# Seven products in place of eight in the late matrix products of an attention and PReLU kernel

## The chip, the cores and the metric

The kernel runs on one core of one Trainium2 chip. The metric is device microseconds of one execution, the median of several; lower is better. Work on the core is spread over TensorE (PE, matrix products from SBUF into PSUM), VectorE (DVE), ScalarE (ACT), GpSimd (POOL) and the DMA queues that SyncE (SP) and GpSimd feed. Each engine takes its instructions in the order in which the kernel writes them.

## The reference

A block-wise linear attention with a decay per head, and then two matrix products with a PReLU between them. `lam` has a value per head, `alpha` one per hidden column.

```python
# q, k, v: (4, 8, 768, 64); blocks of 64 positions
Dmask = np.where(rel >= 0, lam ** rel, 0.0)
for b in range(nb):
    intra = einsum('bhij,bhjd->bhid', einsum('bhic,bhjc->bhij', qb, kb) * Dmask, vb)
    inter = einsum('bhid,bhde->bhie', qb * lam_pow, kv_state)
    out[:, :, sl] = intra + inter
    kv_state = lam_block * kv_state + einsum('bhsd,bhse->bhde', kb * rev_pow, vb)
x = out.transpose(0, 2, 1, 3).reshape(3072, 512)
h = x @ w_in                                   # 512 -> 2048
g = np.maximum(h, 0.0) + alpha * np.minimum(h, 0.0)
return g @ w_out                               # 2048 -> 512
```

## The kernel before

The 3072 rows are worked in six chunks of 512 (`c` = 0 to 5). A chunk is two batch entries by 256 positions; positions are taken in pairs, so a row index has a part `e` (even or odd position). Attention is done in 24 units (`n`, four to a chunk: batch entry by half of the heads). The kernel works with blocks of 128 positions, two to a chunk.

For a unit: `cast` brings q and k to float16, a transpose by DMA (`transposes(n, "D")`) or by TensorE puts the head dimension on partitions (`qkT`), `decayed` multiplies q by its decay (`qdT`), `key_decayed` does so with k (`kdec`). Then TensorE computes the scores (`score_products`, L387), VectorE multiplies them by the mask (`masked`, L398), TensorE adds the part from the state (`inter`, L371) and the part from the block (`intra`, L412) in the PSUM tile `acc`, ScalarE copies the result to `xT` (`attended`, L248), and the state `R` is brought forward by `state_products` (L432) and VectorE (`states`, L461). `cluster(old, new)` issues these calls for one unit's end and another's beginning.

For a chunk: `up(c, f)` (L532) makes one of 16 groups of 128 hidden columns, four matmuls of 512 columns; ScalarE writes `relu(-h)` to `m` (L540), VectorE computes `g = oma * m + h` from `m` and the PSUM bank (L549), where `oma` is 1 - alpha. `down(c, t, part, 4)` (L562) makes a quarter of the second product for 128 rows, four matmuls of 512 columns; ScalarE copies the finished bank out (L575), SP's queue stores it. `down_last` (L585) is the same for the last chunk, its last tile in pieces of 256, 128 and 128 columns.

Up to chunk 2's first product the order is a written list of calls; from chunk 3 on a string says where `up` (U) and `down` (D) take turns, with attention put between them (`plan`). PSUM has eight banks: two for `acc`, two for the scores, and four named ones: two "h", "tk" and "op". The caller names the bank that a tile takes.

GpSimd runs many casts, most `key_decayed` and `decayed`, and issues the DMAs that load the weights and `v` with a cast to float16 (`load_v16`). SP issues the other loads, the DMA transposes and the stores.

Of the kernel before, what the change touches and what calls it, by code (L numbers as in the profile page):

```python
# [11 lines left out]
def kernel(  # L12
# [26 lines left out]
    L = 128  # L39
# [18 lines left out]
    ps = ctx.enter_context(tc.tile_pool(name="ps", bufs=1, space=bass.MemoryType.PSUM))  # L58
    h_ps_pool = ctx.enter_context(tc.tile_pool(name="hps", bufs=2, space=bass.MemoryType.PSUM))
# [20 lines left out]
    def load(c, bi, x, half=None, queue="S"):  # L80

        pb, b = c // 2, 2 * (c % 2) + bi
        if (c, bi) not in raws:
            raws[c, bi] = [raw_pool.tile([128, H, 2 * D], fp32, tag=f"{n}raw", name=f"{n}raw") for n in "kqv"]
        heads = ds(0, H) if half is None else ds(4 * half, 4)
        i = "kqv".index(x)
        (nc.gpsimd if queue == "G" else nc.sync).dma_start(
            out=raws[c, bi][i][:, heads, :],
            in_=(k, q, v)[i][b, heads, ds(pb * W, W), :].rearrange("h (p e) d -> p h (e d)", e=2),
        )  # L90
# [4 lines left out]
    def load_win(i):  # L95
        nc.gpsimd.dma_start(
            out=w_in_sb[:, :, ts(i, 512)],
            in_=moe_w_in[:, ts(i, 512)].rearrange("(g p) f -> p g f", p=128),
        )

    def load_win8(i):
        nc.gpsimd.dma_start(
            out=w_in_sb[:, :, ts(i, 256)],
            in_=moe_w_in[:, ts(i, 256)].rearrange("(g p) f -> p g f", p=128),
        )
# [24 lines left out]
    def bank_of(bank, name, dtype=fp32):  # L130
        pool = h_ps_pool if bank == "h" else ps
        return pool.tile([128, CH], dtype, tag=bank, name=name)

    def fill(n, bank="h"):

        t = bank_of(bank, "unread")
# [9 lines left out]
    def tick(n, bank="h", x=ident):  # L146

        t = bank_of(bank, "unread")
# [3 lines left out]
    lam_ps = h_ps_pool.tile([128, CH], fp32, tag="h", name="lam_ps")  # L152
    tick(16, "h", zeros[:, 0:128])
# [8 lines left out]
    rel_f = ps.tile([128, CH], fp32, tag="op", name="rel_f")[:, 0:192].rearrange("p (a j) -> p a j", a=3)  # L162
# [71 lines left out]

    def slopes():
        at = h_ps_pool.tile([128, CH], fp32, tag="h", name="at_ps")
        nc.tensor.transpose(at[:, 0:NF], alpha_sb, ident32)
        nc.vector.tensor_scalar(
            out=oma, in0=at[:, 0:NF], scalar1=-1.0, scalar2=1.0, op0=ALU.mult, op1=ALU.add
        )  # L240
# [13 lines left out]
    def raw_of(n):  # L254
        c, bi, hh = units[n]
        return {
            x + "16": t[:, ds(4 * hh, 4), :].rearrange("p h (e d) -> p e h d", e=2)
            for x, t in zip("kqv", raws[c, bi])
        }

    def cast(n, name, eng):
        t = T.setdefault(n, {})
        if name == "v16":
            t[name] = kv_pool.tile([128, 4, 2, D], fp16, tag=name, name=name)
            c, bi, hh = units[n]
            copy_on(eng, t[name].rearrange("p h e d -> p h (e d)"), raws[c, bi][2][:, ds(4 * hh, 4), :])
# [3 lines left out]
        copy_on(eng, t["qk16"][:, int(name == "k16")], raw_of(n)[name])  # L270
# [14 lines left out]
    def key_decayed(n, eng="G"):  # L285
        hh = units[n][2]
        kr = raw_of(n)["k16"]
# [9 lines left out]
    def casts(n, eng):  # L297
        for name, e in zip(("k16", "q16", "v16"), eng):
            cast(n, name, e)
        key_decayed(n)  # L300

    def transposes(n, eng, decay=True):

        t = T[n]
        qkT = qkt_pool.tile([128, 2, 2, 2, L], fp16, tag="qkT", name="qkT")
        if eng == "D":
            nc.sync.dma_start(
                out=qkT.rearrange("p x e h j -> p (x e h) j"),
                in_=t["qk16"].rearrange("p x e h d -> p (x e h d)"),
                transpose=True,  # L310
            )
        else:
            tp = ps.tile([128, 2, 2, 2, L], fp16, tag="tk", name="tp")
            for x in (1, 0):
                for e in range(2):
                    for hp in range(2):
                        nc.tensor.transpose(
                            tp[:, x, e, hp, :],
                            t["qk16"][:, x, e, ds(2 * hp, 2)].rearrange("p l d -> p (l d)"),
                            ident,  # L320
                        )
            copy_on(eng, qkT, tp)
            t["qps"] = tp[:, 0]
        t["qkT"] = qkT
        if decay:
            decayed(n)

    def transposed(n, x, eng, bank):

        c, bi, hh = units[n]  # L330
        t = T.setdefault(n, {})
        if "qkT" not in t:
            t["qkT"] = qkt_pool.tile([128, 2, 2, 2, L], fp16, tag="qkT", name="qkT")
        tp = bank_of(bank, "tpx", fp16).rearrange("p (e h j) -> p e h j", e=2, h=2)
        for e in range(2):
            for hp in range(2):
                nc.tensor.transpose(  # L337
                    tp[:, e, hp, :],
                    t["qk16"][:, x, e, ds(2 * hp, 2)].rearrange("p l d -> p (l d)"),
                    ident,  # L340
                )
        copy_on(eng, t["qkT"][:, x], tp)
        if x == 0:
            t["qps"] = tp
# [80 lines left out]
    def state_products(n, kv, fresh, blocks=None):  # L425
        t = T[n]
        for hp in range(2):
            for e in range(2):
                for hl in range(2):
                    for a in blocks or blocks_of(n):  # L430
                        p = ds(a * 64, 64)
                        nc.tensor.matmul(  # L432
                            kv[a][ds(hl * 64, 64), hp, hl, :],
# [7 lines left out]
    def attended(n, eng):  # L441
        co, bo, ho = units[n]
        if co not in XT:
            XT[co] = xt_pool.tile([128, NHP, 2, 2, L], fp16, tag="xT", name="xT")
# [6 lines left out]
    def states(n, kv, blocks=None):  # L451
        c, bi, hh = units[n]
        pb, b = c // 2, 2 * (c % 2) + bi

        def dense():
            for a in blocks or blocks_of(n):
                m = 2 * pb + a
                if m == 0:
                    continue
                for hp in range(2):  # L460
                    nc.vector.scalar_tensor_tensor(  # L461
                        out=R[b, hh, m + 1][:, hp],
                        in0=R[b, hh, m][:, hp],
                        scalar=rdecay[:, 2 * hh + hp : 2 * hh + hp + 1],
                        in1=kv[a][:, hp],
                        op0=ALU.mult,
                        op1=ALU.add,
                    )

        if pb == 0 and (blocks is None or 0 in blocks):  # L470
            nc.scalar.activation(R[b, hh, 1], kv[0], AF.Copy)
        dense()

    def cluster(old, new, eng="A"):

        if old is not None:
            inter(old)
        if new is not None:
            score_products(new)
        if old is not None:  # L480
            intra(old)
        if new is not None:
            state_products(new, kv_acc, old is None)
            masked(new)
        if old is not None:
            attended(old, eng)
        if new is not None:
            states(new, kv_acc)

    def scores(n):  # L490
        score_products(n)
        masked(n)

    def beside(kv, a):

        p = ds(a * 64, 64)
        for hl in range(2):
            nc.tensor.matmul(
                kv[ds(hl * 64, 64), :, 1 - hl, :],
# [6 lines left out]

    def state(n, pair):

# [583 lines left out]
```

## Time and profile before

| | |
|---|---|
| median of three runs | 210.99 us (210.74 to 211.4) |
| profiled execution, first to last instruction (span) | 209.1 us |
| difference between the two | 1.9 us |
| TensorE busy | 204.0 us, 2151 matmuls |
| VectorE busy | 132.4 us, 233 instructions |
| ScalarE busy | 110.8 us, 207 instructions |
| GpSimd busy | 84.3 us, 114 instructions |

The span is one execution seen by the profiler; the runs' times include what lies around it. A row of a group names the line, the engine, the operation, what it writes from what it reads, the shapes and the count; then the busy time in us, the mean of one instruction in ns, the idle time of the engine just before the group's instructions, and what ended it. A row of the timeline has the start and the length in us. In a stretch's row each engine has its busy us and its count of instructions, and the clock is the share of full speed that TensorE was granted.

### The profile page before, as it was taken

The numbers are of one execution on the slowest core, as the hardware profiler recorded it, in microseconds if no ns is written. First come the engines' busy times: TensorE is split into PE (matmuls) and PEld (weight loads), VectorE is DVE, ScalarE is ACT, GpSimd is POOL, SyncE is SP. The second block draws the span as 40 slices with busy tenths as digits, with TensorE's granted clock in tenths as the row PEclk, the third lists the DMA queues.
The fourth block names the chain that finished last, engine by engine and source line by source line (L and its number), as shares of the span: only waits on it lengthen the run. The fifth ranks groups of instructions, "written<-read, shape, count | busy, mean of one in ns | idle before, by whom it ended". The sixth has DMA issues, their size and how long they took to land.

```text
span 209.1 us, 5240 instructions
## 1 busy us (share of the span) xinstructions
PE 204.0 (98%) x2151; PEld 109.3 (52%) x2151; DVE 132.4 (63%) x233; ACT 110.8 (53%) x207; POOL 84.3 (40%) x114
## 2 busy tenths in 40 slices
PE   7999999999999999999999999999999999999993
PEld 6776455456445465555554464544544444444453
DVE  7978889488789466999956656744674344444000
ACT  7986778154876127666844544643454544344121
POOL 8999793052476983381902938022000000000000
PEclk9999999999999999999999999999999999999999
DMA  6999999998999998999199990404110100111113
GB/s 159 277 197 239 245 253 206 241 282 260 269 211 262 196 241 184 252 209 221 28 220 229 298 211 1 103 0 103 50 48 5 50 39 11 53 52 50 51 50 103
DMA packets 56716, 32.20 MB, mean 154 GB/s; under 512 B 22948, under 2 KB 53044, under 8 KB 56692
## 3 DMA queue, kind: packets, MB, share of 16 engines
q1 hardware_dynamic: 45764, 23.34, 46.4%
q0 software_dynamic: 10912, 8.52, 23.4%
q8 instruction: 17, 0.28, 0.6%
q14 instruction: 7, 0.06, 0.1%
q10 hardware_dynamic: 16, 0.00, 0.0%
HBM read 27.27 MB, written 6.29 MB: 161 GB/s over the span
## 4 chain that ended last, share of the span: by engine, by line
PE 92%; DVE 3%; ACT 2%; issue 1%; ACTq 0%
PE h_ps L532 39%; PE o_ps L562 33%; PE o_ps L585 7%; PE s L387 3%; PE acc L412 2%; PE tpx L337 2%; PE acc L371 2%; DVE dmask L200 1%; PE acc L432 1%; PE acc L629 1%; PE acc L615 1%; ACT qk L248 1%; ACT L178 1%; ACT xT L248 1%; DVE kdec L289 1%
## 5 line engine op out<-in xcount | busy, mean ns | idle before, releaser
L549 DVE SCALAR_TENSOR_TENSOR g<-m,oma,h_ps 128x512 f16<-128x512 f32 (+1 forms) x98 | 71.2, 736 | 46.3 <-ACT m L540 43.3
L532 PE MATMUL h_ps<-xT,w_in_sb 128*128 128x512 f16 (+1 forms) x392 | 91.4, 375 | 0.1
L540 ACT ACTIVATE m<-h_ps 128x512 f32<-128x512 f32 (+1 forms) x98 | 57.3, 588 | 51.0 <-PE h_ps L532 50.5
L562 PE MATMUL o_ps<-w_out_sb,g 128*128 128x512 f16 x320 | 79.0, 379 | 0.0
L532 PEld LDWEIGHTS <-w_in_sb 128*128 128x128 f16 x392 | 37.9, 98 | 43.6 <-issue 0.5
L562 PEld LDWEIGHTS <-g 128*128 128x128 f16 x320 | 29.9, 98 | 34.1 <-DVE g L549 0.2
L398 DVE TENSOR_TENSOR sm<-s,dmask 128x1024 f16<-128x1024 f32 x21 | 25.6, 1221 | 12.4 <-PE s L387 11.7
L351 POOL TENSOR_TENSOR qdT<-qkT,qdecay 128x512 f16<-128x512 f16 (+1 forms) x19 | 20.5, 1083 | 17.3 <-PE h_ps L532 7.2
L248 ACT ACTIVATE xT<-acc 128x512 f16<-128x512 f32 (+1 forms) x27 | 14.2, 550 | 22.6 <-PE acc L432 19.4
L575 ACT ACTIVATE o_sb<-o_ps 128x512 f32<-128x512 f32 (+2 forms) x26 | 14.7, 564 | 15.9 <-PE o_ps L585 10.9
L289 POOL TENSOR_TENSOR kdec<-kraw,kdecay 128x512 f16<-128x512 f32 x18 | 19.7, 1102 | 6.0 <-DMA kraw<-in_k_dram 6.0
L461 DVE SCALAR_TENSOR_TENSOR R<-R,rdecay,acc 128x128 f16<-128x128 f16 x54 | 15.3, 342 | 0.0
L252 POOL CAST qk<-qraw 128x512 f16<-128x512 f32 x12 | 7.4, 614 | 17.1 <-DMA qraw<-in_q_dram 16.2
L252 POOL CAST qk<-kraw 128x512 f16<-128x512 f32 x14 | 8.6, 614 | 13.9 <-DMA kraw<-in_k_dram 10.1
L585 PE MATMUL o_ps<-w_out_sb,g 128*128 128x512 f16 (+2 forms) x96 | 14.1, 308 | 0.0
L585 PEld LDWEIGHTS <-g 128*128 128x128 f16 x96 | 8.1, 98 | 6.1
L387 PE MATMUL s<-qkT 64*64 64x128 f16 x336 | 8.8, 221 | 0.1
L276 POOL DMA_DIRECT2D v<-in_v_dram x11 | 8.6, 792 | 0.0
L248 ACT ACTIVATE qk<-qraw 128x512 f16<-128x512 f32 x11 | 6.9, 624 | 2.7 <-DMA qraw<-in_q_dram 2.1
L252 POOL CAST v<-vraw 128x512 f16<-128x512 f32 x10 | 6.1, 615 | 5.4 <-DMA vraw<-in_v_dram 5.4
L387 PEld LDWEIGHTS <-qkT 64*64 64x64 f16 x336 | 5.8, 106 | 2.1 <-issue 0.4
L248 ACT ACTIVATE qkT<-tpx 128x512 f16<-128x512 f16 x11 | 6.5, 598 | 0.8 <-PE tpx L337 0.8
(76 smaller groups left out, 133.5 us busy)
## 6 DMA issues: line engine op xcount, KB each, us to landing
out_dram<-o_sb SPq DMA_DIRECT2D x23, 256.0 KB, 2.3
kraw<-in_k_dram SPq DMA_DIRECT2D x7, 512.0 KB, 5.6
qraw<-in_q_dram SPq DMA_DIRECT2D x6, 512.0 KB, 5.9
w_in_sb<-in_moe_w_in_dram POOLq DMA_DIRECT2D x4, 512.0 KB, 8.0
w_out_sb<-in_moe_w_out_dram POOLq DMA_DIRECT2D x4, 512.0 KB, 10.6
vraw<-in_v_dram SPq DMA_DIRECT2D x7, 256.0 KB, 5.7
qraw<-in_q_dram POOLq DMA_DIRECT2D x6, 256.0 KB, 7.2
qraw<-in_q_dram SPq DMA_DIRECT2D x6, 256.0 KB, 4.8
```

Of the source, the lines that this page charges most:

```text
L248: nc.scalar.activation(out, in_, AF.Copy)
L252: nc.gpsimd.tensor_copy(out=out, in_=in_)
L289: engine(eng).tensor_tensor(out=kdec, in0=kr, in1=kdecay[:, ds(4 * hh, 4), :].rearrange("p h e -> p e h").unsqueeze(3).to_broadcast([128, ...
L351: engine(eng).tensor_tensor(out=qdT[:, :, :, p], in0=(t["qps"] if eng == "P" else t["qkT"][:, 0])[:, :, :, p], in1=qdecay[:, hh, :, :, p], ...
L387: nc.tensor.matmul(t["s"][ds(a * 64, 64), hl, hp, 1 - e, :].rearrange("p (e j) -> p e j", e=2), lhsT=t["qkT"][p, 1, e, hp, ds(a * 64, 64)] ...
L398: nc.vector.tensor_tensor(out=t["sm"].rearrange("p a h x j -> p (a h) x j"), in0=t["s"].rearrange("p a h x j -> p (a h) x j"), in1=mask_of ...
L461: nc.vector.scalar_tensor_tensor(out=R[b, hh, m + 1][:, hp], in0=R[b, hh, m][:, hp], scalar=rdecay[:, 2 * hh + hp : 2 * hh + hp + 1], in1= ...
L532: nc.tensor.matmul(h_ps[:, 0:n] if bi is None else h_ps[:, 0:n].rearrange("p (e j) -> p e j", e=2), lhsT=w_in_sb[:, gi, ts(f, 128)], rhs=x ...
L540: nc.scalar.activation(m[:, 0:n], h_ps[:, 0:n], AF.Relu, scale=-1.0)
L549: nc.vector.scalar_tensor_tensor(out=g, in0=mv, scalar=oma[:, f : f + 1], in1=hv, op0=ALU.mult, op1=ALU.add)
L562: nc.tensor.matmul(o_ps, lhsT=lhs(c, f, t), rhs=w_out_sb[:, f, :], start=(f == 0), stop=(f == NF - 1),)
L585: nc.tensor.matmul(o_ps[:, 0:n], lhsT=lhs(c, f, t), rhs=w_out_sb[:, f, ds(x, n)], start=(f == 0), stop=(f == NF - 1),)
```

## The change

Up to the end of chunk 0's second product the calls stay in their order. `up` is cut into `up`, `relu` and `prelu`, `down` into `down`, `down_copy` and `down_store`, `cluster` into its calls, so that the list can put each on its own place. From chunk 1's first product on the list is a new one, to the end of the kernel.

PSUM's four named banks become one pool of four (`bank_pool`), from which a tile takes whichever has come free. After the attention `acc` and the scores' banks are given back and make a second pool of four (`late_bank`).

Chunks 2 to 5's second product is done by Strassen's scheme in Winograd's form. A quarter of `g` is eight of the 16 groups (`x`) by one `e` (256 rows); `w_out` is cut into halves by hidden row and by output column. `g_sum` forms the sums of the quarters of `g`, half a quarter (128 x 1024, float16) at a time, eight calls to a chunk, all but one sum in the place of a quarter; `w_sum` forms four sums of quarters of `w_out` (128 x 2048) once. A product `second(c, i, b)` is eight matmuls of 256 columns for 128 rows; seven `i` by two `b` make a chunk. The products are added in two PSUM banks, `a` and `e`; `second_m` copies the first out on ScalarE, `second_m5`, `second_x` and two `second_out` are float32 additions of a PSUM bank and a tile in SBUF on VectorE, two `second_out` are copies on ScalarE. Chunk 5's last product is in pieces (`last`), its final columns 128 wide.

Chunks 4 and 5's first product is done as one, 1024 columns wide: seven products for each of eight pairs of column groups (`first(f, i)`, two matmuls of 512 columns each). `in_sum` and `x_sum` form the sums of quarters of `w_in` and of the two chunks' `xT`, four calls each; per `f` there are two copies on ScalarE (`first_b`, `first_m5`) and two additions on VectorE (`first_x`, `first_d`). `first_d` leaves its sum in SBUF; for seven of the eight `f` the `prelu` that follows is two instructions on GpSimd.

`v` of the units from 16 on is loaded with the cast, and no longer cast by an engine. The sums of weights, of `xT` and of chunk 5's `g` use the places of raw inputs and of weights that are no longer read.

```diff
-    ps = ctx.enter_context(tc.tile_pool(name="ps", bufs=1, space=bass.MemoryType.PSUM))
-    h_ps_pool = ctx.enter_context(tc.tile_pool(name="hps", bufs=2, space=bass.MemoryType.PSUM))
+    bank_pool = ctx.enter_context(tc.tile_pool(name="bank", bufs=4, space=bass.MemoryType.PSUM))
+    ps_stack = ctx.enter_context(ExitStack())
+    ps = ps_stack.enter_context(tc.tile_pool(name="ps", bufs=1, space=bass.MemoryType.PSUM))
...
+    def prelu(c, f, bi=None, eng="V"):
+        g, m, h = g_of(c, f), M[c, f, bi], HP[c, f, bi]
...
+        if eng == "G":
+            nc.gpsimd.tensor_scalar(out=m, in0=m, scalar1=oma[:, f : f + 1], scalar2=None, op0=ALU.mult)
+            nc.gpsimd.tensor_tensor(out=g, in0=m, in1=h, op=ALU.add)
+            return
         nc.vector.scalar_tensor_tensor(
+            out=g, in0=m, scalar=oma[:, f : f + 1], in1=h, op0=ALU.mult, op1=ALU.add
         )
...
+        if i == 1:
+            sub(T_OUT[1], b12, b11, eng)
+        elif i == 2:
+            sub(T_OUT[2], b22, T_OUT[1], eng)
+        elif i == 3:
+            sub(T_OUT[3], b22, b12, eng)
+        else:
+            sub(T_OUT[4], b21, T_OUT[2], eng)
...
+        s1 = S1[c][:, ds(4 * j, 4)]
+        if i == 1:
+            add(s1, a21, a22, eng)
+        elif i == 3:
+            sub(a21, a11, a21, eng)
+        elif i == 2:
+            sub(a11, s1, a11, eng)
+        else:
+            sub(a12, a12, a11, eng)
...
+    def second(c, i, b):
+
+        if i in (1, 5) and b == 0:
+            Y[c, "ae"[i == 5]] = late_bank("y") if c == 5 else bank_of("y")
+        t = Y[c, "ae"[i in (3, 5)]]
+        for f in range(8):
+            nc.tensor.matmul(
+                t[:, ds(b * HALF, HALF)],
+                lhsT=left(c, i, f, b),
+                rhs=right(i, f),
+                start=(f == 0 and b == 0 and i in (1, 5, 6)),
+                stop=(f == 7),
+                skip_group_check=True,
             )
...
+        copy_on("A", Y[c, "m1"], Y[c, "a"])
+
+    def second_m5(c):
+        add(Y[c, "m15"], Y[c, "e"], Y[c, "m1"])
+
+    def second_x(c):
+        add(Y[c, "e"], Y[c, "a"], Y[c, "m15"])
+
+    def second_out(c, i):
+        o = SB[c, i] = o_pool.tile([128, DM], fp32, tag="osb", name="o_sb")
+        if i in (2, 3):
+            copy_on("A", o, Y[c, "ae"[i == 3]])
+        else:
+            add(o, Y[c, "a"], Y[c, "m15" if i == 7 else "m1"])
...
+    def first(f, i):
+
+        k = {1: "a", 2: "a", 5: "e", 3: "e"}.get(i, "b")
+        if i in (1, 5):
+            Q[f, k] = late_bank(k)
+        t = Q[f, k]
...
+        for g in range(2):
+            w, x = both(f, i, g)
+            nc.tensor.matmul(
+                t, lhsT=w, rhs=x, start=(g == 0 and i in (1, 5)), stop=(g == 1), skip_group_check=True
+            )
+
+    def first_b(f):
+        Q[f, "b"] = bank_of("b")
+        copy_on("A", Q[f, "b"], Q[f, "a"])
+
+    def first_m5(f):
+        M5[f] = half_pool.tile([128, CH], fp32, tag="qk16", name="m5")
+        copy_on("A", M5[f], Q[f, "e"])
+
+    def first_x(f):
+        add(Q[f, "e"], Q[f, "b"], M5[f])
+
+    def first_d(f):
+        HP[5, 8 + f, None] = m_pool.tile([128, CH], fp32, tag="m", name="d")
+        add(HP[5, 8 + f, None], Q[f, "b"], M5[f])
...
+    up(3, 9)
+    states(16, (0,))
+    relu(3, 9)
+    second(2, 1, 0)
+    g_sum(2, 1, 1)
+    second(2, 1, 1)
+    masked(17)
+    load_v16(22)
+    prelu(3, 9)
+    up(3, 2)
+    inter(16)
+    g_sum(2, 2, 0)
```

In the stages that the prediction names, chunk 1's second product and chunk 2's first run with units 9 to 16 (to chunk 3's first `up`), chunk 2's second and chunk 3's first with units 16 to 23 (to `first(1, 1)`), the joint first product with chunk 3's second (to `second(4, 1, 0)`), and the second products of chunks 4 and 5 close the kernel.

More of the change, by code (lines that the diff above doesn't have):

```diff
@@ L449, in attended, with kv_of, first_state, states @@
         )
-    def states(n, kv, blocks=None):
+    KV = {}
+    def kv_of(n, a):
+        return KV.get((n, a), kv_acc[a])
+    def first_state(n):
+        c, bi, hh = units[n]
+        nc.scalar.activation(R[2 * (c % 2) + bi, hh, 1], kv_of(n, 0), AF.Copy)
+    def states(n, blocks):
         c, bi, hh = units[n]
         pb, b = c // 2, 2 * (c % 2) + bi
[L455 to L472, printed above, removed]
@@ new lines @@
+    prelu(4, 1)
+    second(3, 1, 0)
+    relu(5, 0)
+    first(1, 6)
+    first(2, 1)
+    second_out(2, 4)
+    second(3, 1, 1)
+    prelu(5, 0)
+    first_b(2)
+    first_d(0)
+    first_x(1)
+    first(2, 2)
+    relu(5, 8)
+    prelu(5, 8, None, "G")
+    first(2, 5)
+    x_sum(4)
+    prelu(4, 0)
+    first_m5(2)
+    first(1, 3)
+    g_sum(3, 1, 1)
+    second_m(3)
+    first(1, 7)
+    relu(5, 1)
+    g_sum(3, 3, 0)
+    first_d(1)
+    prelu(5, 1)
+    first(0, 4)
+    first(3, 1)
+    first(2, 6)
```

1533 lines of the change are left out of this document (1041 added, 492 removed).

## The prediction

> **What bounds the kernel now.** I read the page's totals and chain first, then busy time by stretch, then the chain in order of time, then groups by shape.
>
> ```profile
> span 209.1 us, 5240 instructions
> ...
> PE 204.0 (98%) x2151; PEld 109.3 (52%) x2151; DVE 132.4 (63%) x233; ACT 110.8 (53%) x207; POOL 84.3 (40%) x114
> ...
> PE 92%; DVE 3%; ACT 2%; issue 1%; ACTq 0%
> ```
>
> TensorE is busy for 98% of the span and is 92% of the chain that ended last. VectorE is the next engine. The stretches show where each has room:
>
> ```profile
> core 0: us, PE busy (x) PEld busy (x) DVE busy (x) ACT busy (x) POOL busy (x), PEclk, DMA share, GB/s
> 0.00:52.10 52.10, 50.21 (x740) 31.36 (x741) 41.86 (x83) 34.21 (x69) 35.10 (x56) 1.00 1.17 236
> 52.10:70.40 18.30, 18.30 (x137) 9.07 (x136) 16.01 (x28) 12.19 (x23) 12.79 (x16) 1.00 1.21 251
> 70.40:205.90 135.50, 135.44 (x1276) 68.86 (x1274) 74.50 (x123) 64.16 (x114) 36.44 (x45) 1.00 0.47 112
> 205.90:209.10 3.20, 0.02 (x1) 0.00 (x0) 0.00 (x0) 0.28 (x1) 0.00 (x0) 1.00 0.15 44
> ```
>
> Chunk 1's first product starts at 52.1; the last matmul ends at 205.9; the last copy and store take 3.2. The granted clock is 1.00 throughout. VectorE has 61 of 135.5 us free from 70.4 on.
>
> ```profile
> 82.11 4.32 PE h_ps L532 x20
> ...
> 90.90 0.22 PE acc L371 x4
> 91.12 0.35 PE s L387 x16
> 91.47 0.22 PE acc L412 x16
> 91.69 0.12 PE acc L432 x16
> ...
> 192.03 13.91 PE o_ps L585 x96
> ```
>
> Twenty 512-wide matmuls take 4.32, so 0.216 each and 0.865 for a group of four; one unit of attention takes 0.22 + 0.35 + 0.22 + 0.12 = 0.91. From 52.1 on the old kernel has 80 groups of `up`, 80 of `down` and 16 units: 160 x 0.865 + 16 x 0.91 = 153.0, against 153.8 measured. The stretch is dense; only fewer columns can shorten it.
>
> **TensorE after the change.** L585 is 48 matmuls of 512 columns, 16 of 256 and 32 of 128. With a cost of a per column and b per matmul, 512a + b = 0.216 and 48 x 0.216 + 8192a + 48b = 13.91 give 0.42 ns and 2.7 ns, so 0.109 for 256 columns. Chunks 2 to 5's second products lose 4 x 64 matmuls of 512 (55.3) and get 4 x 112 of 256 (49.0): -6.3. Chunks 4 and 5's first products lose 128 of 512 and get 112: 16 x 0.216 = -3.5. Together -9.8, and a TensorE that never waits would end the span at 199.3.
>
> **What VectorE must do for it.** The page's durations overlap in a row of instructions, so I price by starts:
>
> ```profile
> 85.22 0.68 DVE L351 TENSOR_TENSOR qdT<-qkT,qdecay 128x512 f16<-128x512 f16 x1
> 85.83 2.06 DVE L549 SCALAR_TENSOR_TENSOR g<-m,oma,h_ps 128x512 f16<-128x512 f32 x3
> 87.80 1.22 DVE L398 TENSOR_TENSOR sm<-s,dmask 128x1024 f16<-128x1024 f32 x1
> 88.93 1.12 DVE L461 SCALAR_TENSOR_TENSOR R<-R,rdecay,acc 128x128 f16<-128x128 f16 x4
> 89.96 2.35 DVE L549 SCALAR_TENSOR_TENSOR g<-m,oma,h_ps 128x512 f16<-128x512 f32 x3
> ...
> 98.88 2.72 DVE L549 SCALAR_TENSOR_TENSOR g<-m,oma,h_ps 128x512 f16<-128x512 f32 x4
> ```
> ```profile
> L549 DVE SCALAR_TENSOR_TENSOR g<-m,oma,h_ps 128x512 f16<-128x512 f32 x94 | 69.5, 747 | 46.3 <-ACT m L540 43.3
> L658 DVE TENSOR_TENSOR sm<-s,dmask 128x512 f16<-128x512 f32 x6 | 3.8, 682 | 0.0
> L250 DVE COPY qkT<-tpx 128x512 f16<-128x512 f16 x5 | 1.9, 419 | 0.0
> L250 DVE COPY qkT<-tp 128x1024 f16<-128x1024 f16 x1 | 0.7, 686 | 0.0
> L351 DVE TENSOR_TENSOR qdT<-qkT,qdecay 128x512 f16<-128x512 f16 x1 | 0.7, 684 | 0.0
> L351 DVE TENSOR_TENSOR qdT<-qkT,qdecay 128x256 f16<-128x256 f16 x3 | 1.2, 415 | 0.0
> L351 POOL TENSOR_TENSOR qdT<-qkT,qdecay 128x512 f16<-128x512 f16 x15 | 17.4, 1163 | 17.3 <-PE h_ps L532 7.2 <-DMA qkT<-qk 6.6 <-PE acc L615 3.3
> ```
>
> A prelu costs (2.72 - 0.747)/3 = 0.66, a mask 1.13, a state update 0.26, and the next instruction starts about 0.08 before a long one ends. The new float32 adds from PSUM are like L658: 0.682 - 0.08 = 0.60. The sums of float16 quarters are not in this trace. From above: L351, whose `qdecay` operand is float32, grows by (684 - 415)/256 = 1.05 ns per element, so 1024 elements would take 1.22 and 2048 2.30. From below: the all-float16 copy grows by (686 - 419)/512 = 0.52 ns, so 0.69 and 1.22. The new sums are all float16 with runs of 256 elements or more, so I take the copy's row: 0.60 and 1.14 by starts. [...]
>
> I counted the written order in four stages, marked by calls on TensorE, from `w_sum(1)`, which stands 18.3 of TensorE's work behind 52.1 (at about 70.4):
> - A, to chunk 3's first `up`: TensorE 29 groups and 6 units, 30.7. VectorE 17 prelus 11.2, 7 masks 7.9, 24 state updates 6.2, `w_sum` 1 to 3 3.4, two `g_sum` 1.2, a cast and two decays 1.9: 31.8.
> - B, to `first(1, 1)`: TensorE 16 ups, 13 half products of 0.87, 8 units less a few pieces, 31.2. VectorE 15 prelus 9.9, 7 masks 7.9, 16 updates 4.1, four sums of 2048 4.6, eight of 1024 4.8, three adds 1.8: 33.1.
> - C, to `second(4, 1, 0)`: TensorE 110 matmuls and 15 half products, 36.9. VectorE 22 prelus 14.5, 15 `first_x` and `first_d` 9.1, twelve sums of 1024 and one of 2048 8.3, five adds 3.1: 35.0.
> - D, to `second(4, 4, 0)`, which needs the last `g_sum`: TensorE 17.9. VectorE 14 `g_sum` 8.4, 5 prelus 3.3, seven adds 4.2: 15.9. After it TensorE has 7.0.
>
> The room that was 45% of the stretch is gone. In A and B VectorE has 1.1 and 1.9 more than TensorE, and its queue is in order: a prelu late behind a `w_sum` is late for the bank that the next `up` takes. That adds 3.0. C and D have 1.9 and 2.0 to spare, which covers them; were VectorE's prices 10% higher, A and B would add 3.2 and 3.3 more and C 1.6.
>
> **The port.** The new sums read two operands from SBUF. The old trace has VectorE and GpSimd in each other's way:
>
> ```profile
> 44.53 1.04 POOL L289 TENSOR_TENSOR kdec<-kraw,kdecay 128x512 f16<-128x512 f32 x1 [1.04 <-DMA kraw<-in_k_dram]
> ...
> 46.34 0.61 POOL L252 CAST qk<-qraw 128x512 f16<-128x512 f32 x1 [0.76 <-PE tpx L337]
> ...
> 68.53 1.90 POOL L289 TENSOR_TENSOR kdec<-kraw,kdecay 128x512 f16<-128x512 f32 x1
> ```
> ```profile
> 44.56 1.30 DVE L250 CAST qk<-kraw 128x512 f16<-128x512 f32 x1
> ...
> 46.38 0.84 DVE L250 CAST qk<-kraw 128x512 f16<-128x512 f32 x1
> ```
> ```profile
> L250 DVE CAST qk<-qraw 128x512 f16<-128x512 f32 x1 | 0.4, 419 | 0.0
> L289 DVE TENSOR_TENSOR kdec<-kraw,kdecay x6: 677/682/1148, 5.4 to 68.8; 128x512 f16<-128x512 f32 x6
> ```
>
> A cast of 0.42 took 1.30 and 0.84 where a GpSimd instruction had started just before, and GpSimd's own 1.04 became 1.90 at 68.53. Over 17 such VectorE instructions (6 casts, 6 `kdec`, 5 `qdT`) the loss is 0.88 + 0.42 + 0.47 = 1.8, or 0.10 each. A and B have 17 new sums and so add the same 1.8; C's 13 lose 1.4 inside its 1.9 of room. The bounds are nothing, and 0.88 each time GpSimd computes (the second rival).
>
> **The rest, at nothing.** ScalarE has 19.8, 18.0, 28.7 and 5.4 in the stages (new copies are like L575 below, 0.6 each), below TensorE everywhere. GpSimd takes seven prelus of two instructions, between 0.61 (the cast) and 1.16 (`qdT`), taken as 1.1: 15.4 in C's 36.9; in A it has 28.0 of 30.7, covered by `kdec` and `qdT` being written units ahead, and worth up to 2 if they come late. One ring of four banks replaces four named ones; in B two are held by chunk 2's products, which leaves two for `up`, as the old loop had, with 17 us of other TensorE work between 16 ups; uncovered it is the queue of VectorE again. Loads and transposes share SP's queue as before, written earlier; a transpose that waits holds up loads that the stage after next reads. The last piece is 128 wide as before, so 3.2 stays.
>
> ```profile
> L575 ACT ACTIVATE o_sb<-o_ps 128x512 f32<-128x512 f32 x23 | 13.7, 597 | 13.6 <-PE o_ps L585 8.6 <-PE o_ps L562 4.9
> ```
>
> **Sum.** 209.1 - 9.8 + 3.0 + 1.8 = 204.1. The timed runs' median, 210.99, lies 1.9 above the span, which gives 206.0.
>
> **Rivals.**
> - TensorE hides it all. VectorE carries its excess from A and B into C and D, which have 3.9 to spare. For it speaks this stretch of the old kernel, where TensorE stayed full beside a VectorE at 20.9 of 22:
>
> ```profile
> 82.00:104.00 22.00, 22.00 (x285) 11.64 (x284) 20.90 (x40) 15.18 (x27) 11.73 (x15) 1.00 0.83 182
> ```
>
>   Against it: few banks, so little can be carried. 199.3 + 1.9 = 201.2. Chance 0.24.
> - The port decides, and it is slower. If a sum loses a whole 0.88, as at 44.56, whenever GpSimd computes (by the count without its DMA issues 23.3 of 30.7 in A, 10.9 of 31.2 in B, 15.4 of 36.9 in C), then 8, 12 and 13 two-operand instructions lose 5.3, 3.7 and 4.8, of which C hides 1.9: 209.1 - 9.8 + 3.0 + 11.9 + 1.9 = 216.1. It decides from (6.8 + 1.9)/33 = 0.26 per instruction on; below, it is the forecast with another size. Chance 0.19. [...]
> - The sums run one element at a time: 36 x 0.54 + 8 x 1.08 = 28 more for VectorE, of which the stages hide next to nothing: about 231. Against it the copy's row. Chance 0.05.
> - The change doesn't do what it says: half-wide matmuls need as many weight loads for half the columns, and lose what Strassen saves. At 0.123 each, 448 take the old 55.3, and 206.0 becomes 212.3. Against it L585's tail, where even the 128-wide ones fit into 13.91. Chance 0.02.
>
> The forecast has 0.50; its own range is 203.5 to 209. With the rivals the range is 201.0 to 212.0, which leaves out the far half of the port's case and the slow sums. A difference of 0.3% is about what these runs can tell from no change. Faster: 0.24 + 0.47 of the forecast's 0.50 + 0.03 of the port's case = 0.74; within 0.3%: 0.07, from the forecast's upper end and the port's lower; slower 0.19, from the port, the slow sums and the half-wide matmuls.
>
> **What would show it.** Right: VectorE above 90% busy from 70 to 185, TensorE with holes that end on `g` or `sm` in A and B, fewer in C, none in D; `g_sum` rows of 0.69, and some of them 0.2 to 0.9 longer beside GpSimd. Wrong: `g_sum` rows near 1.2; TensorE full in A and B (then 201); holes in D or in the last 7 us, where I price none; a GpSimd whose `kdec` or `qdT` is what TensorE waits for.

## The result

The changed kernel takes 222.73 us (median of four runs, 222.13 to 224.42) against 210.87 for the kernel before on the same chip: 1.058 times, with an interval of 1.054 to 1.062. It is slower by 11.9 us where 206.0 was forecast. The profiled execution has a span of 220.4 and took 222.13 in all. One execution of e3 (224.69 at a mean clock of 0.973, the other 220.66 at 0.992) and one of e14 (216.48 at 0.990, the others 213.07 to 213.69 at 0.997 and more) came out slower, and these two are left out of the numbers below.

From the page of the changed kernel (totals, slices, chain):

```profile
PE 201.2 (91%) x2303; PEld 125.5 (57%) x2303; DVE 179.4 (81%) x298; ACT 114.0 (52%) x215; POOL 110.7 (50%) x129
...
PE   8999999999999999999929999999797798699992
...
issue 12%; POOL 10%; PE 7%; DVE 4%; ACT 4%; DMA 2%; POOLq 1%; ACTq 0%; DVEq 0%
```

TensorE fell from 98% busy to 91%, and from 92% of the chain to 7%. The slices of TensorE show one hole (the 2, at 110 to 116) and a row of smaller ones from 154 on (797798699). The busy time by stretch, cut where the prediction's stages begin (chunk 1, A, B, C, D, the end), and then around the hole:

```profile
core 0: us, PE busy (x) PEld busy (x) DVE busy (x) ACT busy (x) POOL busy (x), PEclk, DMA share, GB/s
52.10:69.40 17.30, 16.68 (x176) 8.57 (x175) 12.83 (x23) 12.21 (x24) 12.86 (x16) 1.00 1.21 275
69.40:104.10 34.70, 33.97 (x448) 17.22 (x446) 32.52 (x57) 17.22 (x31) 21.73 (x26) 1.00 0.96 179
104.10:145.10 41.00, 36.22 (x481) 23.41 (x480) 37.35 (x53) 17.57 (x31) 18.34 (x18) 0.92 0.57 100
145.10:188.50 43.40, 38.37 (x232) 22.40 (x231) 36.27 (x57) 25.90 (x48) 19.14 (x13) 1.00 0.10 37
188.50:208.90 20.40, 18.23 (x163) 15.62 (x162) 16.01 (x26) 5.08 (x9) 2.15 (x2) 1.00 0.11 40
208.90:220.40 11.50, 7.34 (x74) 6.35 (x72) 2.94 (x5) 1.46 (x4) 0.00 (x0) 0.99 0.40 138
111.30:115.40 4.10, 0.05 (x1) 0.00 (x0) 4.10 (x4) 1.92 (x4) 4.08 (x5) 0.88 1.32 203
115.40:122.00 6.60, 6.58 (x61) 3.47 (x61) 4.76 (x8) 2.67 (x5) 2.19 (x3) 0.56 0.44 93
```

Against the work that the prediction counted for TensorE:

| stretch | counted | took | more |
|---|---|---|---|
| 52.1 to the end of A | 18.3 + 30.7 | 52.0 | 3.0 |
| B | 31.2 | 41.0 | 9.8 |
| C | 36.9 | 43.4 | 6.5 |
| D | 17.9 | 20.4 | 2.5 |
| end and tail | 7.0 + 3.2 | 11.5 | 1.3 |

The counted stages add up to 2.0 less than the bound of 199.3 that came from the columns, so 23.1 in all stands for 21.1 above that bound. B and C hold 16 of it.

**B.** The timeline of the changed kernel around its hole:

```profile
105.07 1.05 POOL L284 TENSOR_TENSOR kdec<-kraw,kdecay 128x512 f16<-128x512 f32 x1
105.48 2.55 DVE L550 TENSOR_TENSOR s<-g,g 128x1024 f16<-128x1024 f16 x1
...
110.00 2.85 POOL L284 TENSOR_TENSOR kdec<-kraw,kdecay 128x512 f16<-128x512 f32 x2
...
110.42 1.53 DVE L547 TENSOR_TENSOR g<-g 128x1024 f16<-128x1024 f16 x1
...
111.87 2.83 DVE L547 TENSOR_TENSOR t<-w_out_sb,t 128x2048 f16<-128x2048 f16 x1
...
114.63 1.39 DVE L517 SCALAR_TENSOR_TENSOR g<-m,oma,h_ps 128x512 f16<-128x512 f32 x2
115.42 1.01 PE L491 MATMUL h_ps<-xT,w_in_sb 128*128 128x512 f16 x2 [4.07 <-DVE g L517]
```

`g_sum` took 2.55 at 105.48 and 1.53 at 110.42, `w_sum(4)` 2.83 at 111.87, each with GpSimd computing beside it; two prelus stood behind them in VectorE's queue, and TensorE waited 4.07 for the bank that they free. After the wait the clock was 0.56 of full speed for 6.6 us, which is 6.6 x 0.44 = 2.9 more. Groups of the same kernel show that these durations are not the sums' own speed:

```profile
L547 DVE TENSOR_TENSOR g<-g,g 128x1024 f16<-128x1024 f16 x8 | 5.3, 680 | 0.0
...
L550 DVE TENSOR_TENSOR s<-w_in_sb 128x2048 f16<-128x2048 f16 x1 | 1.2, 1216 | 0.0
```

Six of the first group and the one of the second ran while GpSimd was idle: 1024 elements took 0.68 and 2048 took 1.22. By the timeline the sums of A and B together took 5.0 longer than that, and the three at 105.48, 110.42 and 111.87 took 4.3 of it. The recorded texts call this loss the port; the runs show that sums took longer beside GpSimd, and not what the two engines share.

**C.** Groups and waits of the whole changed kernel (waits: in total, times, longest):

```profile
L514 POOL TENSOR_SCALAR m<-m,oma 128x512 f32<-128x512 f32 x7 | 12.2, 1748 | 35.9 <-ACT m L504 35.9
L515 POOL TENSOR_TENSOR g<-m,d 128x512 f16<-128x512 f32 x7 | 9.1, 1293 | 0.6
```
```profile
ACT m L504 <- POOL g L515: 14.9, 7, 3.3
...
DVE d L550 <- POOL g L515: 5.5, 5, 1.6
...
PE b L751 <- DVE d L550: 4.7, 4, 2.0
```

GpSimd's prelu took 1.75 + 1.29 = 3.0. It reads `m` and `d`, and both lie in the three slots of the pool of `m`. So ScalarE's next relu and VectorE's next `d` waited for GpSimd, 14.9 and 5.5 in all, and TensorE waited 4.7 for `d`, which frees a bank. The longest of these waits, 1.96, lies just behind C, in D.

### The profile page after: what moved, and what is told of

Its sections match the earlier page's. It is cut to its first block, busy times and chain, and to the rows that moved or that the text cites. A ratio compares the mean times of both kernels' runs of the same rounds, so it can differ in the third digit from the quotient of the medians.

```text
span 220.4 us, 5659 instructions
## 1 busy us (share of the span) xinstructions
PE 201.2 (91%) x2303; PEld 125.5 (57%) x2303; DVE 179.4 (81%) x298; ACT 114.0 (52%) x215; POOL 110.7 (50%) x129
## 5 line engine op out<-in xcount | busy, mean ns | idle before, releaser
L491 PE MATMUL h_ps<-xT,w_in_sb 128*128 128x512 f16 (+1 forms) x264 | 61.8, 380 | 4.1 <-DVE g L517 4.1
L504 ACT ACTIVATE m<-h_ps 128x512 f32<-128x512 f32 (+1 forms) x66 | 38.0, 583 | 31.2 <-PE h_ps L491 29.6
L517 DVE SCALAR_TENSOR_TENSOR g<-m,oma,h_ps 128x512 f16<-128x512 f32 (+1 forms) x66 | 46.3, 725 | 7.0 <-ACT m L504 5.7
L629 PEld LDWEIGHTS <-g 128*128 128x128 f16 x368 | 36.0, 99 | 9.0 <-issue 0.6
L629 PE MATMUL y<-w_out_sb,g 128*128 128x256 f16 x240 | 31.1, 278 | 0.2 <-DVE g L517 0.2
L334 POOL TENSOR_TENSOR qdT<-qkT,qdecay 128x512 f16<-128x512 f16 (+1 forms) x19 | 21.1, 1114 | 20.2 <-DMA qkT<-qk 12.0
L525 PE MATMUL o_ps<-w_out_sb,g 128*128 128x512 f16 x128 | 30.8, 380 | 0.0
L514 POOL TENSOR_SCALAR m<-m,oma 128x512 f32<-128x512 f32 x7 | 12.2, 1748 | 35.9 <-ACT m L504 35.9
L246 ACT ACTIVATE xT<-acc 128x512 f16<-128x512 f32 x24 | 14.3, 597 | 20.4 <-PE acc L415 11.7
L450 DVE SCALAR_TENSOR_TENSOR R<-R,rdecay,acc 128x128 f16<-128x128 f16 x54 | 15.5, 340 | 4.9 <-ACT xT L246 4.8
L525 PEld LDWEIGHTS <-g 128*128 128x128 f16 x128 | 11.5, 98 | 11.9
L629 PE MATMUL y<-t,g 128*128 128x256 f16 x128 | 15.3, 273 | 0.0
L271 POOL DMA_DIRECT2D v<-in_v_dram x19 | 14.9, 790 | 0.0
L354 PE MATMUL acc<-qdT,R 128*128 128x128 f16 x80 | 8.7, 224 | 1.7 <-DVE R L450 0.7
```

Of the source, the lines that this page charges most:

```text
L246: nc.scalar.activation(out, in_, AF.Copy)
L334: engine(eng).tensor_tensor(out=qdT[:, :, :, p], in0=(t["qps"] if eng == "P" else t["qkT"][:, 0])[:, :, :, p], in1=qdecay[:, hh, :, :, p], ...
L450: nc.vector.scalar_tensor_tensor(out=R[b, hh, m + 1][:, hp], in0=R[b, hh, m][:, hp], scalar=rdecay[:, 2 * hh + hp : 2 * hh + hp + 1], in1= ...
L491: nc.tensor.matmul(h[:, 0:n] if bi is None else h[:, 0:n].rearrange("p (e j) -> p e j", e=2), lhsT=w_in_sb[:, gi, ts(f, 128)], rhs=x.rearr ...
L504: nc.scalar.activation(m[:, 0:n], HP[c, f, bi][:, 0:n], AF.Relu, scale=-1.0)
L514: nc.gpsimd.tensor_scalar(out=m, in0=m, scalar1=oma[:, f : f + 1], scalar2=None, op0=ALU.mult)
```

## The experiments

Two causes were to be told apart first, one for each of B and C. In brackets stands the ratio to the kernel before, timed beside each run on its chip, with its interval. e1 to e8 were run twice, the others four times.

### The sums and GpSimd in A and B

```diff
# e5_no_sums_ab
 def w_sum(i):
+    if i != 3: use a quarter of w_out in place of the sum
+    return
 def g_sum(c, i, j):
+    if c == 2: return
# e6_gpsimd_quiet
 def key_decayed(n):
+    if n in (16, ..., 21): take unit 22's tile; return
 def decayed(n):
+    if n >= 17: take unit 16's tile; return
```

> Leaves out VectorE's sums for chunk 2's second product and of w_out (w_sum 1 to 4 and the eight g_sum of chunk 2; the products read the quarters unsummed), 9.4 us of VectorE by 1.14 and 0.60. TensorE's work is the same. In the four runs so far VectorE is busy without a break from 83 to 115 us, chunk 3's second stage starts at 105.8 to 110.6 and first(1, 1) at 142.4 to 146.7, against 133 for a TensorE that never waits. Theory E (a full VectorE, with or without the port, is what TensorE waits for in stages A and B): first(1, 1) starts at 134 to 136, no wait over 1 us, clock 1.00. Rival F (banks, or attention's own chain through ScalarE and GpSimd, hold TensorE): first(1, 1) stays at 140 or later.

> Leaves out GpSimd's key decays of units 16 to 21 and query decays of units 17 to 23 (their products read unit 22's and 16's), 13 instructions and 14 us, nearly half of what GpSimd does from 90 to 135 us. VectorE's and TensorE's instructions are the same. Theory C (the shared port is what fills VectorE): the sums of 1024 fall to 0.69 each and first(1, 1) starts at 136 to 138. Theory E without the port (VectorE's own work is too much): first(1, 1) starts at 140 to 142, since the port costs only the 3 to 5 us by which its sums were too long.

e5 measured 215.63 (1.022 times before, 1.012 to 1.032); C's first matmul stands at 137.58 in place of 145.15. e6 measured 215.98 (1.023, 1.016 to 1.031), the same matmul at 139.21. Both matmuls stand between the two forecasts. Taking every sum of chunk 2 and of `w_out` away gives 7.6 us, and leaving the sums but taking GpSimd's instructions from beside them gives 5.9 of these. In e6 the sums run at their own speed, all but `w_sum(3)` (2.5, beside the GpSimd work that is left), the clock stays at 1.00, and no wait in A or B is longer than 0.52:

```profile
L556 DVE TENSOR_TENSOR s<-g,g 128x1024 f16<-128x1024 f16 x3 | 2.0, 679 | 0.0
```

What GpSimd costs the sums beside it is the larger part of what B lost, 5.9 of the 7.6, if the 2.9 of the clock behind the long wait is counted with it; the sums' own time on VectorE accounts for the 1.6 between e5 and e6 and for no more. One caution: e6 also spares the readers of these tiles, so 5.9 is an upper bound for this cost alone. And in e5, with none of these sums, C still begins 5.3 later than the 52.1 + 18.3 + 30.7 + 31.2 = 132.3 that was counted.

```diff
# e3_no_four_kdec
 def key_decayed(n):
+    if n in (17, 18, 19, 20): take unit 21's tile; return
# e4_wsum4_late
-    w_sum(4)
 ...
     prelu(3, 13)
+    w_sum(4)
```

> Leaves out the key decay of units 17 to 20 on GpSimd (their state products read unit 21's), so that GpSimd does no such work around 105 to 112 us; VectorE's instructions are the same. In the changed kernel a float16 sum of 1024 takes 2.55 us there, one of 2048 2.83, TensorE waits 4.1 us for the prelu behind them and then has a clock of 0.56 for 6.6 us. Theory C (the port that VectorE's two-operand sums share with GpSimd): the two sums fall to about 0.7 and 1.2, the wait shrinks to under 1.5 us, the clock stays 1.00, stage B (from chunk 3's first up to first(1, 1)) falls from 41.1 to 35 or less, the span to about 214. Rival D (VectorE simply has too much to do there): the sums shorten but the wait stays at 3 us or more, and stage B at 39 or more.

> Only w_sum(4) is moved, from before prelu(3, 1) to before second(2, 3, 0), where GpSimd has nothing to do. Theory C: the sum takes 1.2 us there, the wait of 4.1 us shrinks to about 1, the clock no longer drops, and the span falls by 4 to 7 us to 213 to 216. Rival D (too much work for VectorE in the stage): TensorE waits as long elsewhere, and the span falls by less than 1.5 us.

e3 measured 220.66, 2.1 below the changed kernel. At the place of the long wait the sums took their own time and the wait was 0.22 in place of 4.07, as Theory C has it. But the next sum met GpSimd's query decays, took 2.27, and a wait of 1.48 came behind it, as the timeline of e3 shows:

```profile
111.21 1.22 DVE L550 TENSOR_TENSOR t<-w_out_sb,t 128x2048 f16<-128x2048 f16 x1
...
113.13 1.02 PE L494 MATMUL h_ps<-xT,w_in_sb 128*128 128x512 f16 x4 [0.22 <-DVE g L520]
...
115.31 2.27 DVE L550 TENSOR_TENSOR g<-s,g 128x1024 f16<-128x1024 f16 x1
```

C began 2.8 earlier, and a fall of the clock at 188 to 193 cost 1.7 of this again, behind a wait of 1.95 that the changed kernel has too (1.96), without a fall. e4 measured 221.05 (1.046, 1.028 to 1.065), with C's first matmul at 145.14, where it was. Moving one sum moved the wait: in e4 `w_sum(3)` met GpSimd instead, and the timeline shows how a sum loses.

```profile
97.21 1.04 POOL L284 TENSOR_TENSOR kdec<-kraw,kdecay 128x512 f16<-128x512 f32 x1
97.59 4.99 DVE L547 TENSOR_TENSOR w_out_sb<-w_out_sb 128x2048 f16<-128x2048 f16 x1
98.20 0.60 POOL L250 CAST qk<-kraw 128x512 f16<-128x512 f32 x1
98.77 1.15 POOL L334 TENSOR_TENSOR qdT<-qkT,qdecay 128x512 f16<-128x512 f16 x1
99.88 0.60 POOL L250 CAST qk<-kraw 128x512 f16<-128x512 f32 x1
100.45 1.04 POOL L284 TENSOR_TENSOR kdec<-kraw,kdecay 128x512 f16<-128x512 f32 x1
```

The sum of 1.22 took 4.99: five GpSimd instructions in a row ended before it did, and TensorE waited 2.61 behind it. Over the runs, where the list up to there is the same, this one sum took between 1.2 and 5.0, so how much a sum lost was in part luck. There was no single price per instruction; at worst, as here, a sum lost 3.8, nearly the whole 3.9 from its start to the end of the fifth. It did not end between these GpSimd instructions, which follow each other closely; at 110.42 in the changed kernel one ended while the second of two `kdec` was still under way.

### The slots in C

```diff
# e1_prelu_vector, seven times (f = 8 to 14)
-    prelu(5, f, None, "G")
+    prelu(5, f)
# e2_sum_tile_apart
 def first_d(f):
-    ... = m_pool.tile([128, CH], fp32, tag="m", name="d")
+    ... = sm_pool.tile([128, CH], fp32, tag="sm", name="d")
```

> The seven prelus that GpSimd does in the joint first product go back to VectorE; nothing else is changed. The changed kernel spends 43.4 us from first(1, 1) to second(4, 1, 0) on 36.9 us of TensorE work, and GpSimd's pair of instructions takes 2.8 to 3.5 us where I had priced 2.2. Theory A (GpSimd's slow pair, in the chain between ScalarE's relu and the three shared m tiles, stretches this stage): the stage falls to about 40 (VectorE's 36.3 busy plus seven prelus of 0.66, less its waits of 7 us for GpSimd and ScalarE), the span from 220.4 to about 217. Rival B (VectorE bounds the stage): the 4.6 us that VectorE gets lengthen the stage to 46 or more, the span to 223.

> GpSimd keeps its seven prelus, but the sum that it reads (first_d's tile) lies in a pool of its own that the attention has left, no longer among the three m tiles. Theory A2 (it is not GpSimd's duration as such but the m tiles that it holds for 3 us: ScalarE waits 14.9 us and VectorE 5.5 us for GpSimd's g): most of these waits go, the stage falls from 43.4 to 38 to 39, the span to about 216. Rival (each prelu pair lies on a chain of data): the waits stay over 10 us and the stage over 42.

e1 measured 217.68 (1.031, 1.015 to 1.046), e2 217.39 (1.029, 1.023 to 1.035). The stage to `second(4, 1, 0)` took 39.5 and 40.0 in place of 43.4, and from the first matmul of the joint product to the last, which reaches into D, they took 41.6 and 40.8 where the changed kernel took 46.4. So e1's rival, which had the stage lengthen, is out. In e2 GpSimd is as slow as before, and ScalarE still waits for it, over 10 us as that run's rival had it, but the stage is under its 42:

```profile
ACT m L504 <- POOL g L515: 11.4, 7, 2.8
```

TensorE's waits for `d` fell from 4.7 to 0.8. What cost 5.6 us was not GpSimd's speed but the slots that it kept from `d`; with the slots apart, whether GpSimd or VectorE does the seven prelus makes no clear difference (e2 against e1 here, e9 against e11 below).

### Parts undone

```diff
# e7_chunk2_plain: chunk 2's second product as before
-    second(2, i, b), g_sum(2, i, j) and what belongs to them
+    down(2, t, p) at the same places, with down_copy and down_store
     g_sum(3, 3, 0)
+    w_sum(3)
# e8_first_plain: the joint first product as before
-    first(f, i), first_b, first_m5, first_x, first_d, in_sum, x_sum
+    up(4, f), up(5, f) at the places where their banks became ready
```

> Undoes one part: chunk 2's second product is plain (16 quarters of four matmuls of 512), its eight g_sum, three additions and the ScalarE copy are gone, w_sum(3) comes in chunk 3's product, and chunk 1's stores are issued where their copies are. TensorE gets 1.6 us more, VectorE 6.6 us less before first(1, 1). Theory E: first(1, 1) starts at 137 to 139 in place of 142 to 147 and the span is 213 to 216: the part costs more than it saves. Rival F: TensorE's 1.6 us are added, the span is 221 or more.

> Undoes another part: chunks 4 and 5's first products are plain, 32 groups of four matmuls in the places of the joint product's calls, all prelus on VectorE, no in_sum, x_sum, first_x, first_d, and ScalarE's 16 copies gone. TensorE gets 3.5 us more, VectorE 12.2 us less (16.8 of sums and additions, plus seven prelus), GpSimd 21 less. Theory A: the stage from first(1, 1)'s place to second(4, 1, 0), 43.4 us now, takes 40.5 to 41.5, TensorE's new bound, and stage B loses its in_sum and x_sum, so the span is 213 to 216. Rival: the stage stays over 43, since VectorE was not what it waited for.

e7 measured 220.42 (1.044, 1.028 to 1.061), between the two forecasts: C began only 2.3 earlier. The sums left in it lost at most 0.2 each, but the stores of chunk 1, which had to be written earlier in SyncE's list, held up the transposes, and TensorE waited 1.43 for `qkT` at 105. e8 measured 217.29 (1.030, 1.020 to 1.039), above its 213 to 216, but as much below the changed kernel as e1 and e2, and that with 3.5 us more columns: with its slots in the way, the joint product was a loss.

### Both causes taken away

```diff
# e9_plain2_sum_apart = e7 with chunk 1's stores later, and e2
# e10_second_3_4_5_only = e7 with chunk 1's stores later, and e8
# e11_plain2_apart_vector = e9 and e1
```

> Chunk 2's second product plain, its two chunk-1 stores later in SyncE's list, and the joint product's sum d in a tile of its own (the two edits with a gain so far, together). Theory A (two separate causes: VectorE's sums of chunk 2 beside GpSimd, and the slots that GpSimd holds in stage C): they add up, and the wait for qkT at 105 is gone too: 220.4 - 5.5 - 1.5 = about 213.5 (212 to 215), stage C 41. Rival (both loosen one and the same chain, or another wait of the list holds the time): not below 216.

> As e9, but the joint first product undone as well (plain ups of chunks 4 and 5, prelus on VectorE): only the second products of chunks 3, 4 and 5 are Strassen's. TensorE then saves 3 x 1.6 = 4.8 us of columns against before. Theory A (what costs the time is chunk 2's sums and the joint product's slots): 210.9 - 4.8 + up to 6 of waits, 207 to 212, at or below before. Rival (the new order of the list from chunk 1 on costs time whatever is multiplied): 213 or more.

> As e9, with the seven prelus of the joint product on VectorE instead of GpSimd. Theory A (GpSimd's pair of 3.0 us is late for its waiters): 0.5 to 1.5 us below e9. Rival (with the slots apart, it is VectorE's time that counts in stage C): 1 to 3 us above e9.

e9 measured 213.47 (1.012, 1.009 to 1.014), e11 213.25 (1.011, 1.008 to 1.014): the two causes add up, as expected, and 9.3 us come back. e10 measured 214.75 (1.018, 1.014 to 1.021), as its rival had it, though it has 4.8 us fewer columns than the kernel before and neither chunk 2's sums nor the joint product. Its profile has TensorE's clock at 1.00 to the last matmul and no wait over 0.9. So a third cost was left. With its slots apart the joint product gains 1.3 (e9 against e10) of the 3.5 that its columns promise.

### The list and the banks alone

```diff
# e12_second_4_5_late_sums = e10, and
-    second(3, i, b), g_sum(3, i, j) and what belongs to them
+    down(3, t, p) at the same places
-    w_sum(1), w_sum(2), w_sum(4) where they stood
+    w_sum(1) to w_sum(4) around second(4, 1, 0) and second(4, 5, 0)
# e13_joint_4_5_late_sums = e12 with e11's joint first product
```

> As e10, but chunk 3's second product plain too, and all four sums of w_out (w_sum 1 to 4) moved out of 70 to 115, to where chunk 4's second product begins: up to about 155 the changed list then runs nothing but plain products. In e10, by the counts of TensorE's instructions at full clock, 62 to 92 and 112 to 132 hold about 6 us less work than the same stretches of before. Theory L (the new order of the list with its ring of PSUM banks costs these 6 us whatever is multiplied): they stay, 210.9 - 3.3 + 6.5 = 213 to 216. Rival S (the sums of w_out on VectorE are late there): the holes close, 207 to 210.

> As e12, with the joint first product kept (its sum d in a tile of its own, its prelus on VectorE): some 3.5 us fewer columns than e12, and in e9 against e10 1.3 us of it was seen. Theory L: 211 to 215. Rival S: 204 to 209, below before.

e12 measured 216.39 (1.028, 1.025 to 1.030), e13 216.96 (1.032, 1.027 to 1.036), above the range of theory L by 0.4 and 2.0 and far from rival S. Up to `second(4, 1, 0)`, which starts at 181.51 in e12, TensorE computes nothing but plain products, in the new list with the new ring of banks. From chunk 1's first matmul at 51.92 it has 126 groups of 0.865 and 15.5 units of 0.91 to do, 123.1 us, so it could be there at 175.0: the list and the ring lose 6.5 us. By the same count the kernel before loses 0.8 over all of its 153.8, and its profile lists no wait of TensorE there. With e5's 5.3 up to C this agrees in size. (The rest of e12 is not to be read in this way, since its moved sums stand in the way behind 181; so they do in e13, where TensorE waits 2.71 for `d` at 185.) TensorE's waits in e12 from 52 to 181:

```profile
PE acc L354 <- ACT xT L246: 1.0, 2, 0.8
PE h_ps L491 <- DVE g L517: 0.5, 2, 0.2
PE acc L354 <- DVE R L450: 0.4, 2, 0.2
PE acc L354 <- POOL qk L250: 0.3, 1, 0.3
PE s L370 <- DMA qkT<-qk: 0.3, 1, 0.3
```

They come to 2.5, in 8 waits. A wait cost more here than its number, and a unit of attention more than its 0.91, as the timelines of e12 and then of the kernel before show:

```profile
87.39 0.39 PE L354 MATMUL acc<-qdT,R 128*128 128x128 f16 x4
...
88.18 1.04 PE L491 MATMUL h_ps<-xT,w_in_sb 128*128 128x512 f16 x4
89.15 0.42 PE L370 MATMUL s<-qkT 64*64 64x128 f16 x16
89.50 3.63 PE L491 MATMUL h_ps<-xT,w_in_sb 128*128 128x512 f16 x16
...
122.42 1.03 PE L491 MATMUL h_ps<-xT,w_in_sb 128*128 128x512 f16 x4
123.62 0.38 PE L354 MATMUL acc<-qdT,R 128*128 128x128 f16 x4 [0.18 <-DVE R L450]
```
```profile
90.74 0.39 PE L371 MATMUL acc<-qdT,R 128*128 128x128 f16 x4
...
91.75 1.04 PE L562 MATMUL o_ps<-w_out_sb,g 128*128 128x512 f16 x4
```

A group's row is 1.03 long, but the next started 0.865 after it when nothing was waited for (98.76 behind 97.89). At 123.62 the next starts 1.20 later: a wait of 0.18 lost 0.34. By the same count the six others that follow a group of `up` or `down` lost 0.15 to 0.17 more than they print. So the 8 waits lose 2.5 + 8 x 0.16 = 3.8. The old list issued a unit's four pieces in one go, which took 91.75 - 90.74 = 1.01 from start to start, so the 0.91 was too low by 0.10; here the scores stand apart, one `up` later, and the pieces take 88.18 - 87.39 = 0.79, 89.50 - 89.15 = 0.35, and 0.10 by which the `up` between them is longer: 1.24. Over the whole stretch 129.6 - 109.0 - 3.8 = 16.8 are left for the units, 1.08 each, or 2.7 more than 15.5 x 0.91. The low price makes 1.6 of that and the cutting into pieces up to 1.1; this 2.7 is what is left over, not a measurement of every unit.

```diff
# e14_moved_calls = e11, and
-    attended(16), states(10), states(12), w_sum(3) where they stood
+    each ahead of the call that made it late (w_sum(3) behind first_d(1))
 def last_copy:  o from the pool of m in place of osb
 second(4, 3, 1) ahead of the last two pieces
```

> As e11, with calls moved that the trace of e11 shows late, one for each wait of TensorE: attended(16) ahead of the copy and relu that kept it from 114.2 to 114.6 (wait 0.80); states(10) ahead of a prelu (0.39); states(12) ahead of a decay that waits for a transpose (0.41); w_sum(3) behind first_d(1) (1.04); and at the end the last copies in m's tiles and chunk 4's last product ahead of the last two pieces (4.0 behind TensorE's end, 3.2 in before). Theory L (the new order loses its time in such single waits of the unit by unit attention and of VectorE's queue): each goes and none takes its place, 213.25 - 0.8 - 0.4 - 0.4 - 1.0 - 0.7 = about 210. Rival (the engines behind are full, and each wait comes back elsewhere): 212 to 213.5.

e14 measured 213.18 (213.07 to 213.69), nothing gained on e11, as its rival had it. The waits of 0.80 at 115 and of 1.04 at 154 went, and others came in their stead, of 1.2 for `e` and of 0.7 for `xT`. So the waits are not a few misplaced calls. Whether they come from the ring of banks, from the units being worked one at a time (the old plan ran them in pairs from chunk 3 on, `cluster2`), or from the order otherwise was not separated. No version tried is below the kernel before; the nearest are e9, e11 and e14, at 213.2 to 213.5.

## Why the prediction was wrong

**What held.** The columns: 32 half-wide matmuls start 3.49 apart in the changed kernel, 0.109 each, as worked out from the old tail.

```profile
205.42 3.66 PE L629 MATMUL y<-w_out_sb,g 128*128 128x256 f16 x32
208.91 3.66 PE L629 MATMUL y<-t,g 128*128 128x256 f16 x32
```

The speed of the sums (0.68 and 1.22), taken from the copy's row against `qdT`'s, held, and so did signs named for A and B: VectorE busy 94% and 91% of them, and a hole in B that ends on `g`. Two signs failed: VectorE was busy 84% of C, not over 90%, and D had a hole of 1.96.

**The port, +1.8: this step failed first.** It took a mean of 0.10 per instruction from 17 old cases. The old cases were casts and decays scattered over the kernel; the new sums stand where GpSimd's instructions come in runs. Of the old loss the six casts, which read one operand, had 1.3 and the eleven `kdec` and `qdT`, which read two, 0.5, so no run shows that it matters how many operands a sum reads. In the changed kernel the sums of A and B lose 5.0, or 0.3 each, in place of 1.8. e6 puts what hung on it in A and B at up to 5.9, with the 2.9 of the clock. The rival named GpSimd and the side, but its price of 0.88 per sum was no bound: the sum at 97.59 in e4 lost 3.8. That its 216.1 was nearer is in part luck, since it held 9.0 for this cost in A and B and nothing for the clock, the slots and the list.

**VectorE's excess, +3.0: right in kind, not in size.** With GpSimd out of the way, taking the sums away as well gave 1.6.

**The clock was not in the sum at all.** The old trace had it at 1.00 throughout the matrix products and had no wait that could show anything else. Behind the 4.07 it cost 2.9.

**GpSimd's prelus "at nothing": failed.** The pair was priced at 2.2 and is 3.0, which was still covered by GpSimd's own room. The cover was the wrong one: the work beside the pair did not matter, the slots did. `d` shares three of them with `m`, and the prediction did not look at who else takes a tile from that pool. C took 6.5 more and D 2.5, of which e2 gives back 5.6, 3.4 of it in C.

**The ring and the list "at nothing": failed.** The prediction counted VectorE's and TensorE's work by stage and took a stage's length from the larger. e12 computes the same products as the kernel before up to 181 and loses 6.5 there, in waits of 0.2 to 0.8, in units cut into more pieces, and 1.6 in the low price of a unit; the waits and the pieces are in no sum by stage. Of the 10.7 that e9 still stands above its own bound (199.3 + 1.6 + 1.9 = 202.8), this is the larger part if e9 loses as much as e12; the forecast had set 4.8 aside for all of it, under VectorE's excess and the port's +1.8.

**D and the tail.** D was forecast without holes and took 2.5 more, with one wait of 1.96 for `d` from C; the tail is 4.1 in place of 3.2. There the first of the last copies waits for a tile whose store is not done (ScalarE idle until 213.93), and ScalarE makes a 512-wide copy ahead of the last one; which of these costs the 0.9 was not separated.

## What to carry to other kernels

To price VectorE's sums beside GpSimd, look at how long GpSimd works without a gap where they will stand, not at a mean over the old trace: here the mean was 0.10 per instruction, and the sum at 97.59 in e4 lost 3.8 to a stretch of 3.9. Before putting a new user on a pool or an engine, list who else takes a slot from that pool and how long the slowest holder keeps it; speed was not what mattered here, the slot was (5.6 us in e2). And a new order of calls is a change of its own: run it once with the old arithmetic before its savings are counted, since TensorE lost 3.8 us in e12 in waits of 0.2 to 0.8, seven of the eight with 0.15 to 0.17 more than the profile prints, and up to 1.1 in work cut into smaller pieces.

## What the runs showed of the hardware

The clock fell behind single waits of TensorE, the shortest of them 1.95 us. In e8 TensorE waited 2.23 us, up to 117.58, and these are the stretches around its end:

```profile
115.00:117.60 2.60, 0.37 (x3) 0.09 (x2) 2.60 (x3) 0.60 (x1) 2.60 (x2) 1.00 1.09 150
117.60:119.60 2.00, 2.00 (x11) 1.26 (x11) 2.00 (x4) 0.86 (x2) 0.28 (x1) 0.77 0.01 2
119.60:121.60 2.00, 2.00 (x7) 0.79 (x6) 2.00 (x4) 0.82 (x2) 0.00 (x0) 0.50 0.00 0
121.60:123.60 2.00, 2.00 (x49) 1.36 (x48) 1.12 (x3) 1.46 (x3) 1.23 (x2) 0.88 0.95 295
```

The granted clock was 1.00 during the wait, 0.77, 0.50 and 0.88 in the stretches of 2.0 behind it, and then 1.00 again: 0.46 + 1.00 + 0.24 = 1.7 us more for a wait of 2.23. From 52 on, in the traces of all runs, all seven waits of 2.06 and more were followed by such a fall: 1.7 more each behind the 2.06 and 2.50 of e1, the 2.24 of e2, the 2.23, the 2.61 of e4 and the 2.71 of e13, and 2.9 behind the 4.07. None of 1.56 or less was. In between stands one wait for `d`, of 1.95 or 1.96, that six traces share, and it goes either way: the clock fell behind it in e3, e5 and e7 and not in the changed kernel, e4 and e6. The stretch of 4.0 behind it in e5 and then in e6:

```profile
184.00:188.00 4.00, 4.00 (x22) 2.82 (x22) 3.59 (x6) 2.48 (x5) 0.00 (x0) 0.63 0.01 2
185.60:189.60 4.00, 3.79 (x32) 2.92 (x32) 3.59 (x6) 2.91 (x6) 0.00 (x0) 1.00 0.00 2
```

So the six waits of 2.06 to 2.71 cost 1.7 more than their length here, and the one of 1.95 or 1.96 had a fall behind it in three of six traces. Of e1's two runs the one with the two falls had a mean clock of 0.984 and took 219.06, the other 1.000 and 216.29.
